# Windowed attention and a squared-ReLU product on one core: 192-token units up to token 3072, the rows of x turned by 128-row matmuls over zeros, the second product 15 units behind

## The chip, the core and the metric

One core of a Trainium2 chip runs the whole program. The metric is the device time of one execution in microseconds (us); the published number of a kernel is the median over its runs. The kernel before took 290.09 us (three runs: 293.07, 290.09, 288.38).

## What is computed

For 8 batches of 8 heads, 576 positions and head width 64, attention is taken within a window of 32 positions to either side, and its output, laid out as 4608 tokens of 512 features, goes through two matrix products with a squared ReLU between:

```
mask = np.abs(pos[:, None] - pos[None, :]) <= 32
scores = np.where(mask, q @ k.T / np.sqrt(D), -1e9)
attn = softmax(scores);  x = attn @ v          # x: 4608 tokens x 512
h = x @ w_in                                   # w_in: 512 x 2048
out = np.maximum(h, 0.0) ** 2 @ w_out          # w_out: 2048 x 512
```

## The kernel before, in words

**Attention** goes by groups of 192 positions, three to a batch and 24 in all (G = 0 to 23). A group's q, k and v rows are loaded by POOL's DMA queue with a cast to bf16; q and k are turned so that features lie on the partitions, by matmuls against the identity for G below 6 (`turn_pe`, L578) and by transposing DMAs on SP's queue from G = 6 on (`turn_dma`, L618). Scores are 24 small matmuls on half of the array's rows (L707; L659 for the first groups). ACT takes their exponentials (L721, L724), DVE multiplies by the band mask (L729 for the outer two of the three steps, L735 twice for the middle one), and two groups of eight matmuls (`pv`, L763) multiply by v, the first and the second window of the group. DVE divides by the sums (reciprocal L782, product L785), which gives `xa` (64 token rows, on partitions 64 to 127) and `xb` (128 token rows). `xa` is written in its lower half only; the partitions 0 to 63 of its buffers are never written.

**Turning x** (`xturn`, from L799). For G below 5 the token rows are turned on TensorE, and ACT copies the result to `xt` (L860): L843 turns `xa`, four matmuls of 64 rows by 64 columns, and L848 turns `xb`, four of 128 by 128. G = 0 has a form of its own (L811 to L838). From G = 5 on both are transposing DMAs on SP's queue (L864, L867), so each `xt` row passes two queues before the first product can use it: SP's, where it stands behind the q and k turns that were put there earlier, and the DMA engines'.

**First product** (`mm1`, L889). It goes by tiles of 192 tokens below token 2304 and of 256 tokens from there to 4096 (`TILES`); each tile is 64 matmuls over 16 blocks of `w_in` columns, two blocks to a PSUM bank. ACT applies ReLU (L895), and ACT or DVE squares (L905, L903) into `gt`. The last 512 tokens use a seven-product scheme (`mm1_tile`, `mm1_pair`, L966), for which `setup_w1s` (L922) prepares eight sums of `w_in` halves on DVE and writes them into the buffers that held raw k and q; such a write waits until the last transposing DMA that reads its buffer is done.

**Second product** (`mm2`, L1023; `mm2_pair`, L1083, a seven-product scheme over two blocks of 128 tokens) follows `LAGP` units of 64 tokens behind the first, and its sums go out by DMAs.

**What sets the order.** Each operation is recorded once with a key (its due place, in units of 64 tokens), a duration and what it reads and writes. `Prog.schedule` (L175) then plays the five engines and three DMA queues through a table of costs, takes the ready operation with the lowest key, and so fixes one static order for each engine. ACT or DVE is chosen for operations that have both forms (`alt`, with the offsets of `FLEX`). The keys get small random shifts (`SEEDS`, `NOISE`). Attention of group G is due at `pos(G)` (L471), 3G - 8 less `LGS` for each group after the sixth; the first product of token t0 is due at t0/64 - 1. In the planned gaps of the opening the scheduler places matmuls over zeros that nothing reads (L412). On the chip each engine runs its list in order, so an instruction that waits holds up all that stand behind it.

Of the kernel before, what the change touches and what calls it, by code (L numbers as in the profile page):

```python
# [7 lines left out]
ACTF = mybir.ActivationFunctionType  # L8
# [8 lines left out]
NBLK = NTOK // 128  # L17
# [12 lines left out]
GK = 7.0  # L30
# [4 lines left out]
TBK = 0  # L35
GDL = 1
# [11 lines left out]
LSLACK = 1200  # L48
# [21 lines left out]
LGS = 0.2  # L70
WLEAD = 3
TILES = ((192, 2304), (256, 4608))
SEEDS = (43876, 83318, 97513, 36951, 80411, 85349, 77111, 51195, 76437, 71531, 64050, 49961, 54177, 91158, 55691, 27992, 55556, 58548, 7419, 10134)
NOISE = 0.1
NBIAS = 1
PKEY = 0.2
# [12 lines left out]
LAGP = 14.0  # L89
PSTEP = 0.35  # L90
SLEAD = 1.0
MOE = -1
SQBEG = 576
ULATE = 26
# [3 lines left out]
OFFS = {'S': 2.5, 'M': -2.5, 'g': 2.25, 'Z': 3.25, 'N': -1.75, 'cc.': -3.0, 'u': -2.0, 'X': -0.5, 'r': -2.25, 'c': -1.0}  # L98
DLEAD = 0.3
TWKEY = 7  # L100
# [3 lines left out]
FLEX = {'g': -1.75, 'Z': -2, 'ev': 0.25, 'o': 4.75, 'p': 3.25, 'm': -1.5}  # L104
# [9 lines left out]
class Prog:  # L114
# [45 lines left out]
    def kind(self, op):  # L160
        n = op.name
        return "s" if n[0] == "S" or n[0] == "T" and n[-1] == "a" else "t" if n[0] == "t" else "v" if n[0] == "P" and "." not in n else ""
# [201 lines left out]
class Gen:  # L364
# [434 lines left out]
    def xturn(self, G):  # L799
        xa, xb = self.XA[G % 3], self.XB[G % 3]  # L800
        key = self.pos(G) + 0.5
        r = 192 * G % RING
        wr = [("xt", (3 * G + c) % (RING // 64)) for c in range(3)]
        if G < NXT:
# [35 lines left out]

            def f0(e):
                for j in range(4):
                    mm = e.transpose(ps[:, 192 * j:192 * j + 64], xa[64:128, 128 * j:128 * j + 128], self.ID[64:128, 64:128])  # L843
                return mm

            def f1(e):
                for j in range(4):
                    mm = e.transpose(pb[:, 192 * j + 64:192 * j + 192], xb[:, 128 * j:128 * j + 128], self.ID[:])  # L848
                return mm

            self.p.rec("PE", f0, reads=[("xa", G % 3), "id"], writes=bank, key=key, dur=110, name=f"T{G}a")
            self.p.rec("PE", f1, reads=[("xb", G % 3), "id"] + bank * (not two), writes=bank2, key=key, dur=230, name=f"T{G}b")
            if two:
                for x, (c0, c1) in enumerate(((0, 64), (64, 192))):
# [6 lines left out]
                                                     ps[:, 0:768].rearrange("p (j q) -> p j q", j=4), ACTF.Copy),  # L861
# [314 lines left out]
    def build(self):  # L1176
# [37 lines left out]
        def at(key, f, *a):  # L1214
            todo.append((key, len(todo), f, a))
# [22 lines left out]
        while t0 < NTOK:  # L1238
            if t0 in STR1:
                if t0 == STR1[0]:  # L1240
                    at(t0 / 64 - 2.5, self.setup_w1s, t0 / 64 - WLEAD)
                at(t0 / 64 - 2, self.mm1_tile, t0, t0 / 64 + MOE)
                for d in range(8):
                    at(t0 / 64 + d + MOE, self.mm1_pair, t0, d, t0 / 64 + d + MOE)
                t0 += 512
                continue
            n = next(n for n, end in TILES if t0 < end)
            m = min(512 // n, 4)
            for d in range(0, 16, m):
                key = t0 / 64 + d / 16 * n / 64 + MOE  # L1250
                at(key, self.mm1, t0, n, list(range(d, d + m)), key)
            t0 += n
        if NBLK - 2 not in PAIRS:
            at(500, self.mm2_last, NBLK - 1, 500)
        for u in PAIRS:
            key = 2 * u + LAGP - 4 * (u == NBLK - 2)
# [50 lines left out]
```

## Time and profile before

| | |
|---|---|
| published time | 290.09 us, median of 3 (288.38 to 293.07) |
| the profiled execution, its own time | 291.74 us |
| its span, first to last instruction | 289.9 us |
| granted TensorE clock | 1.00 |
| TensorE (PE) busy | 282.1 us, 97% |
| weight loads (PEld) busy | 245.2 us, 85% |
| VectorE (DVE) busy | 219.8 us, 76% |
| ScalarE (ACT) busy | 215.4 us, 74% |
| GpSimd (POOL) busy | 106.8 us, 37% |
| first matmul over zeros that nothing reads, their number | at 1.2 us, 32 |

A row of the timeline gives the start, the length, the engine, the line and the operation, `out<-in`, the tile shape, how many instructions were merged, and in square brackets how long the engine sat idle before and what it waited for. Matmuls overlap, so the length of a merged row contains the run-out of its last one; the distance from a row's start to the next row's start is what it took of PE. A row of the windows gives, for each engine, the busy time inside the stretch. "DVE L922" in a wait means that DVE's instruction at line 922 was what ended it; "issue" is a wait that the profile puts down to nothing it shows.

### The profile page before, as it was taken

To read this page: it belongs to the slowest core of one execution; us is meant where nothing else is said; L and a number is where in the kernel's file an instruction comes from. 1 tells how busy PE (TensorE), PEld (TensorE's weight loads), DVE (VectorE), ACT (ScalarE), POOL (GpSimd) and SP (SyncE) were. 2 spreads that over 40 slices of the span, in tenths; PEclk is the share of its full clock that TensorE was granted. 3 is DMA by queue.
4 is the path that set the end of the run, shared out by engine and by line. 5 is a ranking of instruction groups with operands and counts; after the bars stand their busy time and mean duration, and the time that the engine had idled before them with its cause. 6 is when DMAs were issued, how large, how long until landed. Compare 5 with 4: busy or idle time off the path is not lost.

```text
span 289.9 us, 8460 instructions
## 1 busy us (share of the span) xinstructions
PE 282.1 (97%) x3424; PEld 245.2 (85%) x3430; DVE 219.8 (76%) x472; ACT 215.4 (74%) x404; POOL 106.8 (37%) x143
## 2 busy tenths in 40 slices
PE   7998999999999999999999899999999999999996
PEld 2567988698899999999988788898889888888885
DVE  6668679969668978688866664987898857889863
ACT  3379999985489889688978898777887855788310
POOL 8985663260264664454665246425000000000000
PEclk9999999999999999999999999999999999999999
DMA  9999999999599999999999999999922030202124
GB/s 167 188 194 176 205 179 161 135 195 132 128 158 179 131 165 141 210 150 134 179 145 188 150 122 186 169 152 187 170 41 84 20 102 0 76 0 76 72 75 145
DMA packets 158983, 39.59 MB, mean 137 GB/s; under 512 B 148320, under 2 KB 154592, under 8 KB 158944
## 3 DMA queue, kind: packets, MB, share of 16 engines
q0 software_dynamic: 106016, 17.93, 89.8%
q1 hardware_dynamic: 47888, 12.07, 31.7%
q10 hardware_dynamic: 5040, 9.05, 10.0%
q8 instruction: 27, 0.44, 0.7%
q14 instruction: 12, 0.10, 0.1%
HBM read 36.70 MB, written 9.44 MB: 159 GB/s over the span
## 4 chain that ended last, share of the span: by engine, by line
PE 87%; DMA 5%; DVE 5%; ACT 2%; issue 1%; DVEq 0%
PE ht L889 32%; PE outp L1083 29%; PE at L1083 6%; PE at L763 4%; DMA xt<-xb 3%; PE at L707 3%; PE outp L1023 2%; PE at L966 2%; PE ht L966 2%; DMA oe<-in_q_dram 1%; PE outp L412 1%; PE outp L889 1%; PE at L889 1%; DVE kt L609 1%; PE at L578 1%
## 5 line engine op out<-in xcount | busy, mean ns | idle before, releaser
L889 PE MATMUL ht<-xt,w 128*128 128x192 bf16 (+1 forms) x1120 | 119.5, 256 | 0.7 <-DMA xt<-xb 0.7
L889 PEld LDWEIGHTS ht<-xt,w 128*128 128x128 bf16 x1120 | 96.6, 98 | 8.0 <-DMA xt<-xb 1.0
L895 ACT ACTIVATE rt<-ht 128x384 bf16<-128x384 f32 (+1 forms) x140 | 72.2, 529 | 21.7 <-PE ht L889 20.6
L905 ACT ACTIVATE gt<-rt 128x384 bf16<-128x384 bf16 (+1 forms) x122 | 67.1, 566 | 2.4
L536 POOL DMA_DIRECT2D v<-in_v_dram x48 | 38.3, 805 | 43.8 <-PE at L763 19.4
L487 POOL DMA_DIRECT2D kraw<-in_k_dram x36 | 28.1, 783 | 36.5 <-issue 14.6
L487 POOL DMA_DIRECT2D qraw<-in_q_dram x36 | 28.1, 782 | 10.3 <-PE ht L889 5.2
L1083 PE MATMUL outp<-w,gt 128*128 128x256 bf16 x224 | 29.0, 273 | 0.0
L1083 PE MATMUL outp<-tw,gt 128*128 128x256 bf16 x224 | 29.0, 273 | 0.0
L1083 PE MATMUL outp<-tw,ss 128*128 128x256 bf16 x224 | 28.9, 273 | 0.1
L1083 PEld LDWEIGHTS outp<-w,gt 128*128 128x128 bf16 x224 | 21.5, 98 | 2.6
L1083 PEld LDWEIGHTS outp<-tw,gt 128*128 128x128 bf16 x224 | 21.7, 98 | 2.3
L1083 PEld LDWEIGHTS outp<-tw,ss 128*128 128x128 bf16 x224 | 21.2, 98 | 2.7 <-DVE ss L1069 0.3
L721 ACT ACTIVATE e<-at 128x1024 bf16<-128x1024 f32 x21 | 21.4, 1021 | 2.1 <-PE at L707 1.9
L763 PE MATMUL at<-v,pt 128*128 128x66 bf16 x384 | 20.1, 194 | 0.5 <-DVE pt L735 0.5
L735 DVE TENSOR_TENSOR pt<-em,mask 64x512 bf16<-64x512 bf16 x42 | 17.6, 420 | 3.8 <-ACT em L724 2.4
L763 PEld LDWEIGHTS at<-v,pt 128*128 128x128 bf16 x384 | 17.9, 98 | 1.7 <-DVE pt L735 0.8
L903 DVE TENSOR_TENSOR gt<-rt 128x384 bf16<-128x384 bf16 (+1 forms) x30 | 11.4, 382 | 10.2 <-ACT rt L895 10.0
L729 DVE TENSOR_TENSOR pt<-e,mask 128x1024 bf16<-128x1024 bf16 x21 | 14.5, 691 | 5.4 <-ACT e L721 5.0
L1103 DVE TENSOR_TENSOR oe<-outp,uu 128x256 f32<-128x256 f32 (+1 forms) x28 | 15.4, 551 | 3.4 <-PE outp L1083 2.8
L785 DVE TENSOR_TENSOR xa<-at,rs 64x512 bf16<-64x512 f32 x24 | 16.7, 695 | 1.1
L785 DVE TENSOR_TENSOR xb<-at,rs 128x512 bf16<-128x512 f32 x24 | 16.5, 686 | 0.7
(151 smaller groups left out, 412.0 us busy)
## 6 DMA issues: line engine op xcount, KB each, us to landing
out_dram<-oe ACTq DMA_DIRECT2D x34, 256.0 KB, 4.6
qraw<-in_q_dram POOLq DMA_DIRECT2D x36, 96.0 KB, 7.3
w<-in_moe_w_in_dram POOLq DMA_DIRECT2D x4, 512.0 KB, 11.0
v<-in_v_dram POOLq DMA_DIRECT2D x16, 128.0 KB, 8.1
w<-in_moe_w_out_dram POOLq DMA_DIRECT2D x4, 512.0 KB, 17.6
v<-in_v_dram POOLq DMA_DIRECT2D x16, 96.0 KB, 7.3
kraw<-in_k_dram POOLq DMA_DIRECT2D x12, 112.0 KB, 7.2
kraw<-in_k_dram POOLq DMA_DIRECT2D x12, 96.0 KB, 7.4
```

Of the source, the lines that this page charges most:

```text
L487: self.p.rec("POOL", lambda e, j=j: e.dma_start(raw[0:h, j, :].rearrange("p (h d) -> p h d", h=8), s[:, j]), writes=[("raw", t, G % NRAW, ...
L536: self.p.rec("POOL", lambda e, j=j, lo=lo, hi=hi, k0=k0: e.dma_start(vt[lo - k0:hi - k0, j, :, 0:64], self.v[b, :, lo:hi, :].rearrange("h ...
L721: self.p.rec("ACT", lambda e: e.activation(e2[:], self.AT[:, 0:1024], ACTF.Exp, scale=0.125), reads=lo, writes=[("e", n)], key=key, dur=ac ...
L729: self.p.rec("DVE", lambda e: e.tensor_tensor(out, e2[:].rearrange("p (h s q) -> p h s q", h=8, s=2), mb, ALU.mult), reads=[("e", n), ("ma ...
L735: self.p.rec("DVE", lambda e, w=w, r=r, x=x, mm=mm: e.tensor_tensor(pt[x:x + 64, w, :, 0:64], e1[r:r + 64, :].rearrange("p (h q) -> p h q" ...
L763: mm = e.matmul(avp[:, c:c + VS], pt[:, 4 * (h % 2) + h // 2, :], vt[:, w, h, :], start=(w == 0 and y == 0), stop=True, skip_group_check=True)
L785: self.p.rec("DVE", lambda e: e.tensor_tensor(x[r0:128, :].rearrange("p (x y c) -> p x y c", x=2, y=4), av[:, :, :, 0:64], rb, ALU.mult), ...
L889: mm = e.matmul(ht[:, n * x:n * x + n], self.W1[:, ft, 128 * d:128 * d + 128], self.XT[:, ft, r:r + n], start=(ft == 0), stop=(ft == 3))
L895: self.p.rec("ACT", lambda e: e.activation(rt[:, 0:c], ht[:, 0:c], ACTF.Relu), reads=htag, writes=[("rt", k % 4)], key=key, dur=act(c), na ...
L905: alt=("ACT", lambda e: e.activation(gt[:, d0:d0 + len(ds), r:r + n], rr, ACTF.Square), act(c), "g")
L1083: mm = e.matmul(op[:, 256 * half:256 * half + 256], a[:, d, :], w[:, d, :], start=first and d == 0, stop=d == 7, skip_group_check=True)
L1103: self.p.rec("DVE", lambda e: e.tensor_tensor(out, src, other, ALU.add), reads=btags[bank] + rd, writes=wr, key=key + k * PSTEP - DLEAD, d ...
```

## The change

- `TILES` gives 192-token tiles up to token 3072, 256-token tiles from there to 4096. The 768 tokens from 2304 on are four tiles of 64 matmuls with 192 columns, where they were three tiles of 64 with 256 columns. A 192-token tile reads the rows of one group; a 256-token tile reads those of two.
- `TFULL`: for groups 1 to 4 `xa` is turned by four full matmuls of 128 rows by 128 columns, over all partitions, whose first 64 output columns are dropped. So that partitions 0 to 63 hold zeros, three operations (`xz0` to `xz2`) clear them once in the opening; in the order they stand on ACT, ahead of what was its first activation before.
- `LAGP` 15 for 14: the second product is due one unit later. `LGS` 0.15 for 0.2: attention is due a little later for late groups. `GK` 6.5 for 7: loads of groups from 12 on are due half a unit later. `WLEAD` 6.5 for 3: the sums of `w_in` halves are due earlier.
- New random shifts, offsets and choices between ACT and DVE. `SQBEG`, `ULATE`, `LAGS` and `KPL` come with values that choose nothing else than before.

```
-GK = 7.0
+GK = 6.5
+TFULL = True
+XZKEY = -5
-LGS = 0.2
-WLEAD = 3
-TILES = ((192, 2304), (256, 4608))
+LGS = 0.15
+WLEAD = 6.5
+TILES = ((192, 3072), (256, 4608))
-LAGP = 14.0
-PSTEP = 0.35
+LAGP = 15
+PSTEP = 0.45
...
+            c = 64 * TFULL
+
             def f0(e):
                 for j in range(4):
-                    mm = e.transpose(ps[:, 192 * j:192 * j + 64], xa[64:128, 128 * j:128 * j + 128], self.ID[64:128, 64:128])
+                    if TFULL:
+                        mm = e.transpose(ps[:, 192 * j:192 * j + 128], xa[:, 128 * j:128 * j + 128], self.ID[:])
...
-                    mm = e.transpose(pb[:, 192 * j + 64:192 * j + 192], xb[:, 128 * j:128 * j + 128], self.ID[:])
+                    mm = e.transpose(pb[:, 192 * j + 64 + c:192 * j + 192 + c], xb[:, 128 * j:128 * j + 128], self.ID[:])
...
-                                                     ps[:, 0:768].rearrange("p (j q) -> p j q", j=4), ACTF.Copy),
+                                                     ps[:, c:768 + c].rearrange("p (j q) -> p j q", j=4), ACTF.Copy),
...
+        for i in range(3 * TFULL):
+            x = self.XA[i][0:64, :]
+            at(-20, lambda i, x: self.p.rec("DVE", lambda e: e.memset(x, 0.0), reads=["zz"], writes=[("xz", i)], key=XZKEY + i, dur=200, name=f"xz{i}",
+                                            alt=("ACT", lambda e: e.activation(x, self.ZZ[0:64, :], ACTF.Copy), 490, "Z")), i, x)
```

Lines after 842 move by up to 14 (L889 becomes L898, L1083 becomes L1092, L922 becomes L931), those before it by 4 (L763 becomes L767).

The change moves instructions on all engines. Three places matter below. The first is PE behind the second `pv` group of G = 14. Before, the last rows ahead of the tile that starts at token 2560 (the last row here), which reads rows that this `pv` leads to:

```order
L889 MATMUL ht<-xt,w 128x256 x16
L1083 MATMUL outp<-tw,ss 128x256 x8
L763 MATMUL at<-v,pt 128x66 x8
L889 MATMUL ht<-xt,w 128x256 x16
L1083 MATMUL outp<-tw,ss 128x256 x8
L707 MATMUL at<-qt,kt 128x64 x24
L889 MATMUL ht<-xt,w 128x256 x8
L1083 MATMUL outp<-tw,gt 128x256 x8
L889 MATMUL ht<-xt,w 128x256 x16
```

and in the change, the rows that start with the second `pv` of G = 15 and end with the row whose last eight matmuls are the first of the tile at token 2688, the first there to read rows of G = 14:

```order
L767 MATMUL at<-v,pt 128x66 x8
L898 MATMUL ht<-xt,w 128x192 x8
L1092 MATMUL outp<-tw,ss 128x256 x8
L711 MATMUL at<-qt,kt 128x64 x24
L898 MATMUL ht<-xt,w 128x192 x16
L1092 MATMUL outp<-tw,ss 128x256 x8
L898 MATMUL ht<-xt,w 128x192 x8
L767 MATMUL at<-v,pt 128x66 x8
L898 MATMUL ht<-xt,w 128x192 x16
```

Between the second `pv` of G = 14 and the first matmul that needs its rows there stood 64 matmuls of 256 columns, 40 of the second product, two groups of scores and two of `pv`; now there stand 104 of 192 columns, 40 of the second product, two of scores and three of `pv`.

The second place is DVE at the second sum of `setup_w1s`, which writes the buffer that held raw k of G = 19. Before, it stood ahead of the masks of G = 18 (L729, L735):

```order
L903 TENSOR_TENSOR gt<-rt 128x2x256
L922 TENSOR_TENSOR kraw<-w 128x1024
L729 TENSOR_TENSOR pt<-e,mask 128x8x2x64
L735 TENSOR_TENSOR pt<-em,mask 64x8x64 x2
L543 COPY v<-v 64x8x64
L1103 TENSOR_TENSOR uu<-outp,uu 128x256
L782 RECIPROCAL rs<-at 64x8
```

and in the change:

```order
L912 TENSOR_TENSOR gt<-rt 128x2x192
L739 TENSOR_TENSOR pt<-em,mask 64x8x64 x2
L733 TENSOR_TENSOR pt<-e,mask 128x8x2x64
L1105 COPY uu<-outp 128x256
L931 TENSOR_TENSOR kraw<-w 128x1024
L786 RECIPROCAL rs<-at 64x8
L1112 TENSOR_TENSOR uu<-outp,uu 128x256
```

The sum now stands behind the masks and ahead of the reciprocal of the same group.

The third place is SP's queue between the turn of `xb` of G = 16 and the turn of `xa` of G = 17. Before:

```order
L867 DMA_TRANSPOSE xt<-xb1 128x4x128
L618 DMA_TRANSPOSE kt0<-kraw1 128x4x96 x2
L618 DMA_TRANSPOSE qt0<-qraw1 128x4x96
L618 DMA_TRANSPOSE qt0<-qraw2 128x4x96
L864 DMA_TRANSPOSE xt<-xa2 128x4x64
```

and in the change:

```order
L876 DMA_TRANSPOSE xt<-xb1 128x4x128
L622 DMA_TRANSPOSE kt0<-kraw1 128x4x96
L622 DMA_TRANSPOSE qt0<-qraw1 128x4x96
L873 DMA_TRANSPOSE xt<-xa2 128x4x64
L622 DMA_TRANSPOSE qt0<-qraw2 128x4x96 x2
L876 DMA_TRANSPOSE xt<-xb2 128x4x128
```

Two turns stand between them where there were four.

More of the change, by code (lines that the diff above doesn't have):

```diff
@@ L35 @@
 TBK = 0
+TFULL = True
+XZKEY = -5
+LAGS = 0.0
+KPL = 0
 GDL = 1
@@ L161, in kind @@
         n = op.name
-        return "s" if n[0] == "S" or n[0] == "T" and n[-1] == "a" else "t" if n[0] == "t" else "v" if n[0] == "P" and "." not in n else ""
+        return "s" if n[0] == "S" or n[0] == "T" and n[-1] == "a" and (not TFULL or n == "T0a") else "t" if n[0] == "t" else "v" if n[0] == "P" and "." not in n else ""
     def change(self, a, b):
@@ L1242, in build @@
                 at(t0 / 64 - 2, self.mm1_tile, t0, t0 / 64 + MOE)
-                for d in range(8):
-                    at(t0 / 64 + d + MOE, self.mm1_pair, t0, d, t0 / 64 + d + MOE)
+                for y in range(2):
+                    for d in range(0, KPL, 2):
+                        for d0 in (d, 8 + d):
+                            key = t0 / 64 + d / 2 - 2 + 0.2 * (d0 > 7) + MOE if y == 0 else t0 / 64 + 8 - KPL / 2 + d / 2 + 0.2 * (d0 > 7) + MOE
+                            at(key, self.mm1, t0 + 256 * y, 256, [d0, d0 + 1], key)
+                for d in range(KPL, 8):
+                    key = t0 / 64 + d - KPL / 2 + MOE
+                    at(key, self.mm1_pair, t0, d, key)
                 t0 += 512
```

24 lines of the change are left out of this document (13 added, 11 removed), and 2 rows, old and new, of the table OPENING.

## Prediction

> **What bounds the kernel now.** I read the page's busy line first, then the stretches, then PE's own waits.
>
> ```profile
> span 289.9 us, 8460 instructions
> PE 282.1 (97%) x3424; PEld 245.2 (85%) x3430; DVE 219.8 (76%) x472; ACT 215.4 (74%) x404; POOL 106.8 (37%) x143
> ```
>
> PE is busy in 97% of the span, and no other engine comes near. A busy PE is not yet an efficient one, so the next views ask where it is not busy, and why.
>
> ```profile
> 0.00:10.00 10.00, 8.20 (x31) 3.39 (x32) 5.83 (x32) 3.41 (x4) 9.03 (x16) 1.00 1.09 173
> 10.00:20.00 10.00, 9.19 (x120) 5.62 (x120) 7.08 (x15) 5.43 (x8) 8.61 (x12) 1.00 1.64 189
> 20.00:30.00 10.00, 9.19 (x139) 8.08 (x137) 8.42 (x19) 9.72 (x19) 6.08 (x9) 1.00 1.77 183
> ...
> 150.00:160.00 10.00, 9.66 (x119) 8.28 (x117) 7.66 (x17) 8.31 (x16) 6.78 (x9) 1.00 1.75 186
> 160.00:170.00 10.00, 9.60 (x119) 8.47 (x120) 6.01 (x14) 8.99 (x17) 4.25 (x7) 1.00 1.87 147
> ...
> 180.00:190.00 10.00, 9.52 (x118) 8.15 (x117) 9.35 (x21) 7.55 (x14) 5.09 (x7) 1.00 2.29 166
> ...
> 280.00:290.00 10.00, 7.14 (x66) 6.17 (x63) 3.32 (x7) 0.77 (x2) 0.00 (x0) 0.99 0.30 107
> ```
>
> After the start, the core and its columns are PE, PEld, DVE, ACT, POOL. Of 289.9 - 282.1 = 7.8 us without PE, the first 30 us hold 1.80 + 0.81 + 0.81 = 3.4, the end 2.8 (the last sums and their stores), the three stretches between 0.34 + 0.40 + 0.48 = 1.2; all others share 0.4. So behind the opening PE can gain little by better order: what it does, it does back to back. The waits name the places.
>
> ```profile
> PE at L843 <- DVE xb L785: 0.8, 1, 0.8
> PE ht L889 <- DMA xt<-xb: 0.7, 1, 0.7
> PE ht L578 <- DVE qraw L510: 0.6, 1, 0.6
> PE at L763 <- DVE pt L735: 0.5, 1, 0.5
> ```
>
> Each is a single wait: for q at the start, for the first turn of x at 26.9 us, and two in the middle, at 160.4 and 181.5. The change can take these and the price of PE's own work; nothing else is open.
>
> **The change part by part.** *192 for 256 columns.* What a matmul takes of PE, from rows of the chain:
>
> ```profile
> 29.55 1.32 PE ht L889 x16
> ...
> 171.50 1.75 PE ht L889 x16
> ```
>
> 1.32/16 = 82.5 ns for 192 columns, 1.75/16 = 109.4 ns for 256. The 768 tokens cost 256 x 82.5 = 21.1 us instead of 192 x 109.4 = 21.0: nothing to gain or lose (+0.1). All other first and second products keep number and shape, so PE's sum of work stands.
>
> *The wait for x at 160.4.*
>
> ```profile
> 146.26 0.42 PE L763 MATMUL at<-v,pt 128*128 128x66 bf16 x8
> ...
> 150.73 1.22 SPq L867 DMA_TRANSPOSE xt<-xb  x1
> ...
> 158.63 1.04 PE L1083 MATMUL outp<-tw,gt 128*128 128x256 bf16 x8
> ...
> 160.40 1.92 PE L889 MATMUL ht<-xt,w 128*128 128x256 bf16 x16 [0.74 <-DMA xt<-xb]
> ```
>
> The second `pv` of G = 14 (146.26) ends at 146.5. Its `xb` was issued at 150.73 and landed at 160.3, 13.8 us after. PE could have begun the tile of token 2560 at 158.63 + 8 x 0.109 = 159.50, 13.0 us after: 0.90 us lost. In the change the first tile that reads rows of G = 14 is that of token 2688. Ahead of it PE has, by the counts shown with the change, 104 x 0.0825 + 40 x 0.109 + 2 x 0.45 + 3 x 0.25 = 14.6 us of work behind that `pv` (a group of scores is 148.36 to 148.81, one of `pv` 146.26 to 146.52 in the timeline). If x takes the same 13.8 us, 0.8 us are to spare and the wait is gone: -0.9 (bounds -0.9 and 0).
>
> *The block on DVE at 180.*
>
> ```profile
> 179.74 0.69 DVE L922 TENSOR_TENSOR kraw<-w 128x1024 bf16<-128x1024 bf16 x1 [3.18 <-issue]
> ...
> 181.06 0.87 DVE L735 TENSOR_TENSOR pt<-em,mask 64x512 bf16<-64x512 bf16 x2
> ...
> 180.02 1.04 PE L889 MATMUL ht<-xt,w 128*128 128x256 bf16 x8
> 181.54 0.43 PE L763 MATMUL at<-v,pt 128*128 128x66 bf16 x8 [0.48 <-DVE pt L735]
> ```
>
> DVE stands 3.18 us at a sum whose buffer SP's turns of k still read, with the masks of G = 18 behind it; PE's `pv` comes 1.52 - 8 x 0.109 = 0.65 us late. In the change the masks stand ahead of that sum: -0.65 (bounds -0.65 and 0). Behind it now waits the reciprocal of the same group, so what is late next is `xa` of G = 18. The tile of token 3456's rows is far off, and I count nothing for it.
>
> *Next to be late.* The first 256-token tile is now that of token 3072, which reads `xa` of G = 17.
>
> ```profile
> 172.90 2.56 SPq L618 DMA_TRANSPOSE qt<-qraw  x2
> 175.56 1.31 SPq L864 DMA_TRANSPOSE xt<-xa  x1
> ...
> 183.55 1.04 PE L889 MATMUL ht<-xt,w 128*128 128x256 bf16 x8
> ...
> DMA to landing us min/median/max: 7.3/7.3/7.3
> ```
>
> It landed at 175.56 + 7.3 = 182.9, and the tile began at 183.55: 0.7 us to spare, 0.65 of it from the wait just removed. By the same count of PE's work the change leaves 10.3 us between the first `pv` of G = 17 and this tile, where there were 11.4. But two turns of SP's queue ahead of it are gone, 2.56 us for two in the row above. Between +1.1 (queue saves nothing) and 0 I take +0.3.
>
> *The turns of x for G = 1 to 4.*
>
> ```profile
> 32.02 1.49 PE L889 MATMUL ht<-xt,w 128*128 128x192 bf16 x16
> 33.44 0.29 PE L843 MATMUL at<-ident,xa 64*128 64x64 bf16 x4
> 33.65 0.40 PE L848 MATMUL at<-ident,xb 128*128 128x128 bf16 x4
> 33.89 0.82 PE L889 MATMUL outp<-xt,w 128*128 128x192 bf16 x8
> ```
>
> Sixteen matmuls take 1.32, here 1.42: going to 64 rows costs 0.10. The four of 64 rows take 0.21, the four full ones 0.24. Two full sets would take 0.48 where 0.10 + 0.21 + 0.24 = 0.55 stand: -0.07 a group, -0.3 in all. The bounds are -0.07 and, if the full set kept the 0.10, +0.03 a group: -0.3 to +0.1. The Trainium skill, page "TensorE: Matmul & The Clock Gate", section "Wait — 56ns, not 53.3ns?", has warm matmuls start N/2.4 GHz + 2.5 ns apart, which the 82.5 ns above meets. By that alone the wider turn costs 4 x (55.8 - 29.2) = 0.11 us a group, +0.4 in all, and the sum below would be 289.2 us for 288.5. That hangs on half-row turns starting 29 ns apart, and the row above shows 0.21/4 = 53 ns.
>
> *The three fills of zeros on ACT.*
>
> ```profile
> 4.95 0.63 ACT L507 ACTIVATE qraw<-oe 96x512 bf16<-96x512 f32 x1 [2.92 <-DMA oe<-in_q_dram]
> ```
>
> ACT idles from 4.95 - 2.92 = 2.03 on for the first load of q. Three fills of 512 columns, at the 0.63 us of the row beside them, take 1.9 and end at 3.9. The cover is this load; without it they would cost 1.9 on the first chain.
>
> *The opening otherwise.*
>
> ```profile
> 10.27 1.16 DVE L609 COPY kt<-outp 128x896 bf16<-128x896 bf16 x1 [1.88 <-PE outp L578]
> 11.41 0.50 DVE L522 COPY kraw<-tw 96x1024 bf16<-96x1024 bf16 x1
> ...
> 12.26 0.51 PE L578 MATMUL outp<-ident,kraw 96*128 96x96 bf16 x8 [0.16 <-DVE mask L445]
> ```
>
> DVE's order now copies this k (L522) in the idle 1.88 us ahead of the first `kt` copy, and the mask's last step is due earlier too, so PE's turn of k need not wait: -0.16 (bounds -0.16 and 0). The order has 31 matmuls over zeros for 32, so the scheduler plans the same holes.
>
> *ACT and DVE.*
>
> ```profile
> L895 ACT ACTIVATE rt<-ht 128x384 bf16<-128x384 f32 x88 | 41.6, 490 | 6.6 <-PE ht L889 6.3
> L905 ACT ACTIVATE gt<-rt 128x384 bf16<-128x384 bf16 x78 | 39.5, 530 | 1.4
> L895 ACT ACTIVATE rt<-ht 128x512 bf16<-128x512 f32 x52 | 30.6, 596 | 15.1 <-PE ht L889 14.3 <-PE at L763 0.5
> L905 ACT ACTIVATE gt<-rt 128x512 bf16<-128x512 bf16 x44 | 27.6, 631 | 1.1
> ```
>
> Thirty-two ReLUs of 0.490 replace 24 of 0.596: +1.4 us; squares alike, 32 x 0.530 - 24 x 0.631 = +1.8, spread over ACT and DVE. That is 3.2 us in about 45, where ACT is busy 8.3 to 9.0 of 10; it fits. Where ACT was busy 9.72 of 10 (20 to 30) PE lost 0.8 to `xb`; if ACT filled up, a like loss per 10 us, up to 3 us, would follow. I take 0. One unit more of lag and later attention move PE's work, not its amount: 0.
>
> The sum: +0.1 - 0.9 - 0.65 + 0.3 - 0.3 - 0.16 = -1.6, so a span of 289.9 - 1.6 = 288.3. This execution took 291.74 us in all, 1.65 above the median of the runs, so the median lies 0.2 above its span: I forecast 288.5 us.
>
> **The rivals.** *The waits only move: 290.1 us.* PE's work is the same, and a new static order with new random shifts has its own late places. For it: the margin at token 3072 is as thin as the two waits that go, and the new sum behind the masks of G = 18 still blocks DVE for as long as SP's turns take. Against: both removed waits have a plain cause that the new order lacks.
>
> *Slower: x lands late in the stage of 192-token tiles, 292.5 us.* Turned x spreads widely:
>
> ```profile
> DMA to landing us min/median/max: 2.5/7.0/9.6
> ```
>
> This is L867 over its 19 turns. Counting PE's work as above, from second `pv` to tile, the tiles of tokens 1152 to 1728 have 9.3 to 13.0 us in the change, 0.8 to 1.6 less than before. From `pv` to issue `xb` of G = 14 took 4.2, so x needs 4.2 + 9.6 = 13.8 at worst. Were all four to meet the worst they would lose 4.5 + 2.3 + 2.1 + 0.8 = 9.7 us; it decides from a landing of about 5 us on at the first and 9 at the last. With under half of that, 4 us, the sum is 288.5 + 4 = 292.5. For it: the slack shrinks there and turns run longer with more in flight. Against: no tile of that stage waited before.
>
> *Much faster: 285.1 us.* If PE's 3.4 us of idle time in the first 30 us went as well, 288.5 - 3.4 = 285.1. The order of the opening, with its 31 matmuls over zeros, says nothing of the kind.
>
> **How the numbers follow.** The forecast gets 0.48, the moved waits 0.28, late x 0.20, much faster 0.04. The unknown terms reach from -2.1 to about +3 round the span; single runs of the kernel before lie 1.7 below and 3.0 above their median. The range 286.2 to 292.6 takes in forecast, moved waits and most of late x. Two per cent, about what a measurement of this kernel can tell from no change, is 5.8 us: below 284.3 or above 295.9. Faster than that 0.03, most of the last case; slower 0.07, the worst third of late x; within 0.90.
>
> **What would show it.** Right: no PE wait on `xt` between 150 and 170 us and none on `pt` near 180, PE busy near 282 us less the fewer fillers, 82.5 ns a matmul up to token 3072, four-matmul turns at 0.24 us. A wait on `xt` at token 3072 above 1 us would break my +0.3. Waits of L898 on DMA `xt` between 75 and 125 us would make the slower rival; ACT above 9.7 of 10 with PE waiting for PSUM would show that the smaller units cost more than their columns.

## The result, and the profile after

| | before | after |
|---|---|---|
| median of the ten runs | 289.69 us (288.38 to 293.07) | 295.79 us (291.26 to 299.44) |
| the profiled execution, its span | 291.74, 289.9 us | 291.61, 289.7 us |
| PE busy | 282.1 us | 282.4 us |

The ratio after to before is 1.010 (95% interval 1.006 to 1.015). A second series of twelve gave a median of 294.76 (288.56 to 300.26) and a ratio of 1.000 (0.9965 to 1.0035). The ratios are formed from the executions near each kernel's fastest only, while every median here is over all of them; so the medians and the shares over 293 us, 16 of 24 executions of the changed kernel against 10 of 125 of the one before, carry what follows. The forecast was 288.5, at most 292.6: wrong.

The profiled execution of the changed kernel is one of the short ones, and in it the forecast's picture holds. Its busy line, the stretches and PE's waits:

```profile
span 289.7 us, 8623 instructions
PE 282.4 (97%) x3487; PEld 247.4 (85%) x3493; DVE 219.6 (76%) x475; ACT 218.3 (75%) x420; POOL 106.9 (37%) x143
...
150.00:160.00 10.00, 10.00 (x143) 9.48 (x141) 6.79 (x16) 8.67 (x18) 5.84 (x9) 1.00 1.80 176
160.00:170.00 10.00, 10.00 (x141) 9.43 (x139) 8.11 (x18) 9.58 (x22) 5.35 (x8) 1.00 1.82 131
...
180.00:190.00 10.00, 10.00 (x126) 8.85 (x124) 8.02 (x17) 9.25 (x18) 4.63 (x6) 1.00 1.91 153
190.00:200.00 10.00, 9.37 (x117) 7.95 (x115) 6.40 (x13) 6.95 (x13) 4.42 (x6) 1.00 1.80 180
```

```profile
PE outp L416 <- DVE zz L410: 1.2, 1, 1.2
PE at L850 <- DVE xb L789: 0.8, 1, 0.8
PE ht L898 <- ACT rt L904: 0.6, 1, 0.6
PE ht L582 <- DVE qraw L514: 0.6, 1, 0.6
```

The three stretches that had 9.66, 9.60 and 9.52 are full; the waits on `xt` and `pt` are gone. One new wait stands at 197 us, for a ReLU on ACT. The time is not in this execution. It shows in a long one: look2, a single execution of the same kernel, 298.23 us. Here are its busy line, the stretches from 140 to 200 us (the last three columns are the granted clock, the DMA share and GB/s) and the longest waits of PE behind the opening:

```profile
span 296.4 us, 8623 instructions
PE 282.2 (95%) x3487; PEld 247.0 (83%) x3493; DVE 219.8 (74%) x475; ACT 219.2 (74%) x420; POOL 106.8 (36%) x143
...
140.00:150.00 10.00, 8.98 (x129) 8.27 (x127) 5.83 (x12) 8.65 (x19) 4.15 (x7) 1.00 2.21 135
150.00:160.00 10.00, 9.54 (x135) 8.82 (x134) 6.73 (x16) 8.14 (x18) 5.21 (x7) 1.00 1.60 165
160.00:170.00 10.00, 9.63 (x136) 8.87 (x134) 7.71 (x17) 9.25 (x21) 4.79 (x8) 1.00 2.29 120
170.00:180.00 10.00, 9.03 (x125) 7.93 (x122) 6.01 (x13) 7.38 (x17) 6.08 (x8) 1.00 1.94 140
180.00:190.00 10.00, 6.05 (x64) 5.12 (x65) 5.61 (x13) 5.18 (x12) 0.71 (x1) 0.92 1.68 167
190.00:200.00 10.00, 10.00 (x116) 8.45 (x115) 6.57 (x13) 7.79 (x14) 3.92 (x6) 0.91 2.50 158
```

```profile
PE ht L898 <- issue: 4.3, 2, 3.8
PE ht L898 <- DMA xt<-xb: 1.4, 2, 1.0
...
PE at L711 <- DVE xb L789: 0.9, 1, 0.9
```

PE is busy as long as in the short execution (282.2 for 282.4) and idle 14.2 us for 7.3. The added idle time, 6.8 us, lies between 140 and 190 us: 5.7 of it are four waits at L898, the first product, and 0.9 is one at the scores (L711). The longest is put down to "issue", that is, to nothing the profile names; the landing of the turned rows names it. PE's rows around it, SP's turn of `xa` of G = 17, and that turn's landing, in the long execution:

```profile
182.35 1.04 PE L1092 MATMUL outp<-tw,ss 128*128 128x256 bf16 x8
187.24 1.03 PE L898 MATMUL ht<-xt,w 128*128 128x256 bf16 x8 [3.85 <-issue]
188.11 0.47 PE L767 MATMUL at<-v,pt 128*128 128x66 bf16 x8
188.39 3.54 PE L898 MATMUL ht<-xt,w 128*128 128x256 bf16 x16
191.77 1.04 PE L1092 MATMUL outp<-tw,gt 128*128 128x256 bf16 x8
...
176.31 1.79 SPq L873 DMA_TRANSPOSE xt<-xa  x1
...
DMA to landing us min/median/max: 10.8/10.8/10.8
```

and in the short one:

```profile
181.12 1.04 PE L898 MATMUL ht<-xt,w 128*128 128x256 bf16 x8
...
172.66 1.19 SPq L873 DMA_TRANSPOSE xt<-xa  x1
...
DMA to landing us min/median/max: 5.3/5.3/5.3
```

The turn is issued 3.7 us later and takes 5.5 us longer: it lands at 187.1, and PE starts the unit of token 3072 at 187.24. In the short execution it lands at 178.0, 3.2 us ahead of need. From the same rows for every unit, the time between the last landing of x and the first matmul that reads it, in us:

| unit of token | 1536 | 1920 | 2304 | 2496 | 2688 | 2880 | 3072 | 3328 |
|---|---|---|---|---|---|---|---|---|
| after, short (289.7) | 4.2 | 3.8 | 5.5 | 5.8 | 6.8 | 4.7 | 3.2 | 3.7 |
| after, long (296.4) | 2.3 | 1.8 | 0.1 | 0.1 | 0.1 | 0.1 | 0.1 | 4.1 |

At 0.1 the unit starts when its rows land.

That the two spans differ by nearly the same 6.7 us is partly chance, since two other differences almost cancel. Behind the long wait sixteen matmuls that else take 1.75 us took 3.38 (188.39 to 191.77), 1.6 us more, at a granted clock near one half. And the short execution lost 1.8 us in the opening, where its matmuls of 512 columns ran at a slower pace, 2.98 us for seven against 1.76. First the short execution, then the long one:

```profile
6.43 3.19 PE L416 MATMUL outp<-zz 128*128 128x512 bf16 x7
9.41 0.95 PE L582 MATMUL outp<-ident,kraw 112*128 112x112 bf16 x8
```

```profile
6.16 1.68 PE L416 MATMUL outp<-zz 128*128 128x512 bf16 x7
7.92 0.57 PE L582 MATMUL outp<-ident,kraw 112*128 112x112 bf16 x8
```

The granted clock reads 1.00 there in both, so the traces do not say why. PE starts the unit of token 0 at 19.4 us in the short execution and at 17.6 in the long one, which up to token 1920 asks for its rows 1.8 us sooner.

SP's queue shows how a late load becomes a late x. SP issues one turn after another: the 60 turns that it starts between 85 and 175 us take it 83 of these 90 us in the short execution. So a turn of k whose rows have not landed holds back all turns behind it, those of x too, and SP has little idle time to catch up. In the long execution:

```profile
SPq L622 <- DMA kraw<-in_k_dram: 4.6, 2, 3.4
```

With 1.6 us booked under another line, SP waits 6.2 us there for loads of k between 60 and 200 us; in the short execution it waits for none. Two of the 6.2 us fall between 115 and 119 us, 3.4 only at 187. At 65 us SP was 1.8 us ahead of the short execution, at 121 us it is 2.7 behind; the other half of that loss is issues that took longer. In the nine profiles below and above that are over 293 us, SP waits for loads of q or k for 2.2 (b_gate) to 9.5 us (again), in the others for 0 to 1.4, but for 4.5 in late. So the question is why loads and turns are late, and what in the change did it.

### The profile page after: what moved, and what is told of

Read it like the earlier page. It is cut to its first block, busy times and chain, and to the rows that moved or that the text cites. A ratio compares the mean times of both kernels' runs of the same rounds, so it can differ in the third digit from the quotient of the medians.

```text
span 289.7 us, 8623 instructions
## 1 busy us (share of the span) xinstructions
PE 282.4 (97%) x3487; PEld 247.4 (85%) x3493; DVE 219.6 (76%) x475; ACT 218.3 (75%) x420; POOL 106.9 (37%) x143
## 4 chain that ended last, share of the span: by engine, by line
PE 90%; DVE 3%; ACT 3%; DMA 1%; ACTq 1%; issue 1%
PE ht L898 34%; PE outp L1092 29%; PE at L1092 6%; PE at L767 4%; PE at L711 3%; PE outp L1032 2%; PE ht L975 2%; PE at L975 2%; PE outp L416 2%; DMA oe<-in_q_dram 1%; PE outp L898 1%; PE at L898 1%; ACTq L1140 1%; PE at L582 1%; ACT qt L610 1%
## 5 line engine op out<-in xcount | busy, mean ns | idle before, releaser
L898 PE MATMUL ht<-xt,w 128*128 128x192 bf16 (+1 forms) x1184 | 119.4, 251 | 0.7 <-ACT rt L904 0.6
L898 PEld LDWEIGHTS ht<-xt,w 128*128 128x128 bf16 x1184 | 99.1, 98 | 6.0 <-ACT rt L904 0.9
L914 ACT ACTIVATE gt<-rt 128x384 bf16<-128x384 bf16 (+1 forms) x120 | 63.9, 551 | 2.6 <-ACT rt L904 0.3
L1092 PE MATMUL outp<-tw,gt 128*128 128x256 bf16 x224 | 29.0, 273 | 0.0
L1092 PE MATMUL outp<-w,gt 128*128 128x256 bf16 x224 | 29.0, 273 | 0.0
L1092 PE MATMUL outp<-tw,ss 128*128 128x256 bf16 x224 | 28.2, 273 | 0.0
L1092 PEld LDWEIGHTS outp<-w,gt 128*128 128x128 bf16 x224 | 21.6, 98 | 2.5
L1092 PEld LDWEIGHTS outp<-tw,gt 128*128 128x128 bf16 x224 | 21.5, 98 | 2.4
L1092 PEld LDWEIGHTS outp<-tw,ss 128*128 128x128 bf16 x224 | 21.2, 98 | 2.4
L739 DVE TENSOR_TENSOR pt<-em,mask 64x512 bf16<-64x512 bf16 x42 | 17.6, 420 | 5.5 <-ACT em L728 4.4
L912 DVE TENSOR_TENSOR gt<-rt 128x384 bf16<-128x384 bf16 (+1 forms) x40 | 14.5, 366 | 8.6 <-ACT rt L904 7.9
L767 PE MATMUL at<-v,pt 128*128 128x66 bf16 x384 | 20.1, 194 | 0.0
L767 PEld LDWEIGHTS at<-v,pt 128*128 128x128 bf16 x384 | 17.7, 98 | 1.8 <-issue 0.5
## 6 DMA issues: line engine op xcount, KB each, us to landing
w<-in_moe_w_out_dram POOLq DMA_DIRECT2D x4, 512.0 KB, 17.6
```

Of the source, the lines that this page charges most:

```text
L739: self.p.rec("DVE", lambda e, w=w, r=r, x=x, mm=mm: e.tensor_tensor(pt[x:x + 64, w, :, 0:64], e1[r:r + 64, :].rearrange("p (h q) -> p h q" ...
L767: mm = e.matmul(avp[:, c:c + VS], pt[:, 4 * (h % 2) + h // 2, :], vt[:, w, h, :], start=(w == 0 and y == 0), stop=True, skip_group_check=True)
L898: mm = e.matmul(ht[:, n * x:n * x + n], self.W1[:, ft, 128 * d:128 * d + 128], self.XT[:, ft, r:r + n], start=(ft == 0), stop=(ft == 3))
L914: alt=("ACT", lambda e: e.activation(gt[:, d0:d0 + len(ds), r:r + n], rr, ACTF.Square), act(c), "g")
L1092: mm = e.matmul(op[:, 256 * half:256 * half + 256], a[:, d, :], w[:, d, :], start=first and d == 0, stop=d == 7, skip_group_check=True)
```

## The experiments

**Is it the kernel, and is it the full-row turns?** Nothing altered, and the turns alone undone in an otherwise identical order on every engine:

```
-  mm = e.transpose(ps[:, 192 * j:192 * j + 128], xa[:, 128 * j:128 * j + 128], self.ID[:])
+  mm = e.transpose(ps[:, 192 * j + 64:192 * j + 128], xa[64:128, 128 * j:128 * j + 128], self.ID[64:128, 64:128])
```

> The changed kernel once more, nothing altered. The profile shown for it has TensorE without the two waits and a span of 289.7 us, yet the median of its runs was 295.8. Theory A (late transfers): most executions have some stages in which rows of x, turned rows of k and q or blocks of v land later than in the profile shown, and TensorE waits 1 to 5 us at a few places; then the median is again 294 to 297 and the profile of a long execution shows waits of TensorE for a DMA that the profile shown does not have. Theory B (granted clock): the same executions show no more waits, but a granted clock under 1.00 for some stretch, and matmuls of 82.5 ns at 192 columns longer there. Theory C: the long executions were of that one chip; then the median here is 290 to 292.

> The changed kernel in its very same order on every engine, with one thing undone: the rows of x of groups 1 to 4 are turned as before by 64-row matmuls of 64 columns instead of 128-row matmuls over zeros (the zero fills stay). If the full-row turns cost what makes the change long (theory D), this one is shorter than the changed kernel by 3 us or more. If late transfers or the order do it (theory A), it is within 1 us of the changed kernel and has the same spread between executions; the forecast's price of the full-row turns (-0.3 us) makes it 0.3 us longer.

> The changed kernel again, one execution and its profile, so that an execution of 294 us or more can be seen beside one of 291. Theory A: waits of TensorE for DMAs (rows of x at the first expert product of 192-token units, turned q or k at the scores) add up to what it is over 291. Theory B: no added waits, a granted clock under 1.00 instead.

> As the look before: one more execution of the changed kernel. If both executions are over 293 us, theory A expects their added waits at the same places in the order (the same groups of rows); theory B expects the granted clock to be low in the same stretch.

Measured: 294.76 us, 7 of 12 over 293; without the full-row turns 294.60, 8 of 12 (before beside them: 289.46, 1 of 23). look1 took 293.75, with one wait of 2.2 us at the unit of token 3072 and the clock at 1.00; look2 is the long execution above. Late transfers (A) hold, the lower clock (B) comes behind them, C and D fall: the turns cost nothing that shows.

**Is it the lag, or the 192-token units?** The order is planned anew in these three:

```
lag14      -LAGP = 15                               +LAGP = 14.0
units2304  -TILES = ((192, 3072), (256, 4608))      +TILES = ((192, 2304), (256, 4608))
b_lag15    -LAGP = 14.0                             +LAGP = 15        (in the kernel before)
```

> The changed kernel with one number back: the second product 14 instead of 15 units behind, all else (192-token units to 3072, full-row turns, weights of the order) as changed. The DMA engines are shown 9 tenths busy or more from the start to 190 us in every profile, and in the changed kernel TensorE starts the units of tokens 1536 to 3584 2 to 4 us earlier than before (103.9 for 105.8, 181.1 for 183.6), so x is needed sooner while the transfers go at the same pace. Theory L (the lag pulls transfer-fed work forward): here the units start 1 to 2 us later than in the changed kernel, the waits for turned x shrink, and the median falls from 295 to 289 to 292 with few executions over 293. Theory S (the 192-token units up to 3072 do it): no change, median 294 to 296.

> The changed kernel with the 192-token units only up to token 2304, as before; the lag of 15 and the rest stay. Theory L: still long, median 293 to 297, with waits for x of 1 us and more at the 256-token units from 2304 on (a 256-token unit needs its last rows of x sooner than a 192-token one). Theory S: the median falls to 289 to 291.

> The kernel before with the lag alone set to 15. Theory L: longer than before, median 291 to 296, with TensorE waiting for turned x between 140 and 190 us in the profile. Theory S, or a third one (the weights and seeds of the order as a whole): within 1 us of before, 288.5 to 290.5.

Measured (before beside them 289.76, 4 of 35 over 293): lag14 293.84, 7 of 12; units2304 291.09, 3 of 12, with five executions from 288.16 to 288.53 and six from 292.50 up; b_lag15 291.20, 1 of 12, without a wait for x. Theory L fell twice: the lag set back does not mend the changed kernel, set forward it does not bring the waits. The median of b_lag15 lies in theory L's range, but not for L's reason: its profile has one added wait, of 1.7 us, at 275 us and for DVE. The units matter, some 4 us in the median, but they are not all of it, since half of the executions of units2304 stay long. What these orders differ in can be counted: second-product matmuls (L1083, L1092) done ahead of the first matmul of the unit at token 1728. In the profiles of before and after:

```profile
0.00:117.60 117.60, 29.76 (x240) 22.76 (x240) 1.00 1.68 164
```

```profile
0.00:113.70 113.70, 26.02 (x208) 19.59 (x208) 1.00 1.70 165
```

240 of them in 117.6 us against 208 in 113.7: all else that PE did up to there is the same to nine matmuls (1472 against 1431 in all). lag14 has 184 (110.5 us), units2304 208, b_lag15 240. The planner, whose keys were all shifted, fills PE differently; the lag's number is only one of its inputs. The count goes with the time only loosely: units2304 has the 208 of the changed kernel and is 4 us shorter, and lag14 with the fewest is not the longest. The next runs intervene.

**Do transfers bind at all?** The order kept, a part of the loads of v left out:

```
-  vt[lo - k0:hi - k0, j, :, 0:64], self.v[b, :, lo:hi, :] ...
+  vt[lo - k0:hi - k0, j, 0:8 if G < 9 else 4, 0:64], self.v[b, 0:8 if G < 9 else 4, lo:hi, :] ...
```

> The changed kernel in its very same order, but from the tenth group of 192 rows on the loads of v bring 4 of 8 heads (the other heads keep older rows, so this leaves out part of the attention's data): about a sixth of the packets on the loads' queue from 79 us on is gone. Theory A (the transfers are at their limit, and whatever is slow in them makes TensorE wait): loads of q and k land 6 to 7 us after issue instead of 9 to 10, no wait of TensorE for x at all, median 287.5 to 289.5 and a spread under 2 us. If the waits come from SP's order rather than from the DMA engines' pace: still 294 to 296.

Measured: 289.16 (288.57 to 290.19), 0 of 12 over 293, ratio 0.9996 (0.9972 to 1.0019); loads of q land 5.1 us after issue, SP waits for none, and PE has no wait on `xt`. That settles the kind of cause: with lighter loads the whole excess goes.

**Does PE come too early for them?** Useless work for PE ahead of the stretch, in the same order:

```
-  for x, d in enumerate(ds):
+  for x, d in list(enumerate(ds)) * (1 + (t0 == 1152 and d0 < 10)):
```

> The changed kernel in its very same order, with 40 first-product matmuls of the unit at token 1152 done twice (their first results are overwritten by the same values): 40 times 82.5 ns, 3.3 us of useless TensorE work at 83 us, ahead of the stretch in which the transfers fall behind. Theory P (in the changed order TensorE reaches the unit of token 1728 at 113.7 us for 117.6 before, with 32 second-product matmuls fewer behind it, 208 for 240, so rows of q, k, v and x are wanted 3 to 4 us sooner than the DMA engines bring them): the added work gives the transfers that time back, the waits for turned x shrink, and the median is 291 to 294, below the changed kernel's 294.8, with the low end at 288.6 + 3.3 = 291.9. If the waits have nothing to do with how far TensorE is ahead of the transfers, 3.3 us come on top: median 298.

Measured: 292.28, five of six between 291.88 and 293.31, one at 297.57 (before 289.05). Adding 3.3 us to the busiest engine shortened the median by 2.5, from 294.76 in an earlier set of runs; before moved by 0.4 between the two sets. The profile is of the one long execution. Its largest wait is not for x, but 2.3 us at the scores, for DVE:

```profile
PE at L711 <- DVE xb L789: 2.3, 1, 2.3
```

```profile
177.48 0.69 DVE L931 TENSOR_TENSOR kraw<-w 128x1024 bf16<-128x1024 bf16 x1 [3.51 <-DMA kt<-kraw]
```

DVE stands 3.5 us at the first sum of `setup_w1s`, whose buffer a late turn of k still reads, with `xb` of G = 17 and the scores behind it. In the short execution this sum does not wait. The 0.9 us at L711 in the long execution above, 1.3 us in gate, the one long wait of late's profile (2.0 us) and that of lag14's (2.6 us, at a later sum) are of the same kind.

**Earlier or later loads.** Each load of q, k and v has, besides its buffer's own hazards, a throttle: it waits for an attention product of an earlier group. The order is kept, and only that wait is moved. `gate` and `b_gate`:

```
+  if op.eng == "POOL" and op.dma is not None and op.dma[0][0] in "qkv" and op.dma[1] > 9:
+      g = self.named[GATE.format(op.dma[1] - GD - GDL)]
+      if g in op.deps:
+          op.deps.discard(g)
+          op.deps.add(self.named[GATE.format(op.dma[1] - GD - GDL - 1)])
```

> The changed kernel in its very same order on every engine; only the throttle of the loads of q, k and v from the tenth group on is one group earlier (a load waits for the second attention product of the group five before it instead of four; the waits for its own buffer stay). Before the stretch in question GpSimd issues no load from 67 to 79 us, and the DMA engines' share falls to 0.8 of 10 there. Theory P: with loads issued in that gap the transfers gain up to 10 us of lead, the waits for turned x go, median 287.5 to 290 and a spread under 3 us. If the DMA engines' pace is not what is short there, or if earlier loads only stand in the way of the turns: 294 or more, the turns landing 9 us and more after issue.

> The kernel before with the same one edit on the throttle of the loads. Its profile shows two waits on that side (0.9 us for turned x at 160 us, 0.65 at 181). Theory P: these go, median 1 to 1.6 us below before, 287.5 to 289. If earlier loads stand in the way of the turns: 290 or more.

> The kernel before, nothing altered, one execution and its profile, to see how the same transfers run there. Theory P: loads of q and k land 6 to 8 us after issue, TensorE reaches the unit of token 1728 at 116 to 118 us, and no wait for x over 1.5 us. If an execution of this kernel has loads at 10 us and waits like those of the changed kernel, the difference between the kernels is one of how often this happens, not of whether.

Two things in these expectations were wrong. The column they read as a share of 10 is the packets' time summed over the queues, in units of the 16 engines' time: 1.6 to 2.3 in the tight stretch, 0.8 in the gap. And groups 10 and 11, whose loads follow that gap, wait for first products and not for the gate's attention products, so the edit left the gap as it was and moved only the loads from group 12 on.

Measured: gate 294.66 (294.39 to 294.98, 6 of 6 over 293), b_gate 294.25 (5 of 6), before 289.05 (0 of 11); b_look 290.56, its unit of token 1728 at 116.1 us, with one wait of 1.7 us for x where none over 1.5 was expected. Loads issued earlier into queues that were already full made gate long in all of its six executions and b_gate in five. In the lists of DMAs (KB, then the median from issue to landing), the changed kernel's short and long executions:

```profile
qraw<-in_q_dram POOLq DMA_DIRECT2D x36, 96.0 KB, 6.7
...
xt<-xb SPq DMA_TRANSPOSE x19, 6.5
```

```profile
qraw<-in_q_dram POOLq DMA_DIRECT2D x36, 96.0 KB, 9.8
...
xt<-xb SPq DMA_TRANSPOSE x19, 8.1
```

and gate:

```profile
qraw<-in_q_dram POOLq DMA_DIRECT2D x36, 96.0 KB, 15.3
...
xt<-xb SPq DMA_TRANSPOSE x19, 7.7
```

Loads that stand longer in their queue go with turns that take longer in theirs, though not evenly (8.1 us at 9.8, 7.7 at 15.3) and not always: in again's profile, the longest of all with a span of 298.4 us, loads of q take 9.6 us and turns of `xb` 5.6, and x is late there because SP issues its turns late, some 6 us behind the short execution's from 147 us on. The loads were then issued earlier where the queues are empty (hole, b_hole), and, the other way, later from group 12 on (late):

```
hole, b_hole
+  if op.eng == "POOL" and op.dma is not None and op.dma[0][0] in "qkv" and op.dma[1] in (10, 11):
+      op.deps = (op.deps - op.raw) | {self.named[GATE.format(op.dma[1] - 5)]}
late
+  if op.eng == "POOL" and op.dma is not None and op.dma[0][0] in "qkv" and op.dma[1] >= GFAR:
+      op.deps = (op.deps - op.raw) | {self.named["P{}A".format(op.dma[1] - 3)]}
```

> The changed kernel in its very same order; only the loads of q, k and v of groups 10 and 11 are issued earlier (they wait for the second attention product of group 5 and 6, at 66 and 75 us, instead of first products at 79 and 86 us), which fills the gap in which the DMA engines idle (0.8 of 10 from 70 to 80 us). From group 12 on the throttle is as it was, so the loads' queue gets no deeper than in the changed kernel. Theory P (the transfers lack the 3 to 4 us by which TensorE runs ahead in the changed order): 12 loads done ahead of the tight stretch give them that back, the waits for turned x shrink to under 2 us, median 288.5 to 291. Theory Q (what slows the turns is how deep the loads are queued, whatever the lead): the queue is as deep as before from 92 us on, so the median stays at 293 to 296.

> The kernel before with the same edit on the loads of groups 10 and 11. Theory P: its two waits (0.9 us for x at 160 us, 0.65 at 181) shrink, median 0.5 to 1.5 us under before. Theory Q: 289 to 290, as before, or up to 293 where the earlier loads leave a deeper queue behind.

> The changed kernel in its very same order; the loads of q, k and v from group 12 on wait for the first attention product of the group three before, about 5 us later than now, so that fewer of them stand in the queue at a time. Theory Q: loads land 5 to 6 us after issue, turns of x 5 to 6 us after theirs, the waits for turned x at 145 to 190 us shrink, median 288.5 to 291 and few over 293. Theory P without Q: loads 5 us later take the last slack (turns of q and k start 0 to 6 us after their rows land), TensorE waits more, median 296 or more.

(late also numbers the semaphores ahead of the loop, since its loads wait for operations that are recorded behind them.) The stretch from 70 to 80 us, in the changed kernel and with the gap filled:

```profile
70.00:80.00 10.00, 10.00 (x127) 8.79 (x125) 7.19 (x15) 4.61 (x10) 0.61 (x1) 1.00 0.81 145
```

```profile
70.00:80.00 10.00, 10.00 (x137) 8.91 (x135) 6.95 (x15) 5.18 (x11) 4.41 (x7) 1.00 1.98 176
```

The DMA share goes from 0.81 to 1.98. Measured: hole 290.36 (289.02 to 293.29, 1 of 12 over 293), ratio 1.0033 (1.0004 to 1.0062); b_hole 289.08 (288.19 to 290.47, 0 of 12), ratio 0.9990 (0.9966 to 1.0014); late 292.71, 3 of 6; before 289.62, 3 of 23. Theory P has its number: twelve loads out of the way ahead of the tight stretch take 4.4 us off the median of the same order (294.76 in the earlier set; before moved by 0.2). In hole's profile SP waits for no load, and one wait for x is left:

```profile
PE ht L901 <- DMA xt<-xb: 0.5, 1, 0.5
```

For theory Q late has the sign, with a median between what the two theories gave. In its profile, the shortest of its six at 291.03, loads land sooner and turns run faster:

```profile
qraw<-in_q_dram POOLq DMA_DIRECT2D x36, 96.0 KB, 6.2
...
xt<-xb SPq DMA_TRANSPOSE x19, 5.2
```

but of the first 14 turns of q and k behind 84 us, eight start within 0.7 us of the landing of their rows (three in the changed kernel's short execution), and half of the executions stay over 293. For b_hole the medians differ by 0.5 us and the interval holds 1: no gain is shown.

**A version that beats both, and what the order is worth without transfers.** units2304 with hole's edit; and the kernel before with light_v's edit:

> The kernel with the 192-token units to 2304 and the rest as changed (median 291.1, its shortest executions 288.2, the longest 295.4), with the loads of groups 10 and 11 issued into the idle gap as in the run that brought the changed kernel from 295 to 290.4. Theory P: the executions of 292 to 295 us go, median 288.2 to 289.5, at or below both kernels. If not, 290 to 292.

> The kernel before with the loads of v cut as in the lighter changed kernel (4 of 8 heads from the tenth group on; it leaves out part of the attention's data). It shows what the change is worth where transfers do not bind: the lighter changed kernel was 289.2 with before at 289.8 beside it. If the forecast's terms on TensorE alone hold (256-column matmuls of 109.4 ns for 192-column ones of 82.5, the turns, the opening: -0.36 us in all, and two waits of 1.55 us that lighter loads take from this kernel too), this one is 288.2 to 289.5, within 0.7 us of the lighter changed kernel. If it is 287.5 or less, the changed order costs TensorE time of its own.

Measured beside before at 289.09 (1 of 23 over 293): hole_2304 289.58 (288.92 to 294.85, 1 of 12), ratio 1.0019 (0.9991 to 1.0046): the executions over 293 go but for one, and what is left is no shorter than before: I have no version that beats both. b_light_v 288.99 (288.31 to 290.77), ratio 0.9995 (0.9972 to 1.0018); light_v had 0.9996. Where transfers do not bind, the two orders take the same time.

## Why the prediction was wrong

**The columns: right.** PE is busy 282.4 us for 282.1, +0.1 forecast.

**The two waits: right as far as they went.** Both are gone from the short execution, and the order of DVE at 180 works as described there. In long executions the same kind of block comes back at the first of these sums (2.1 us of DVE in look2). And the two waits were worth nothing in the median: b_light_v loses its transfer waits too and stands at before's own median, so typical executions of before did not pay the 1.55 us of the one profiled. That one was 1.65 us above the median with a slow opening besides: its unit of token 0 starts at 19.4 us, that of b_look at 17.7. One execution was a poor base to subtract from.

**Turns and opening: too small to see.** The turns' -0.3 had bounds of -0.3 to +0.1; half_turns is 0.16 us off, inside the spread. In the trace the sixteen matmuls ahead of one group's turns take 1.32 us and the two sets 0.23 and 0.22, together 0.10 less than before, where -0.07 was forecast. The wait for the mask is gone, but one of 0.3 us for `qt` has come (L663), and the opening's three stretches keep 3.5 us of idle time for 3.4, so the -0.16 did not come through. The fills of zeros are hidden as said: they end at 3.7 us, ahead of the load.

**The bounds.** Those listed term by term add up to -1.9 and, with the 3 us for ACT, to +4.3, not to -2.1 and about +3; the range ended below its own worst case.

**The step that failed: "One unit more of lag and later attention move PE's work, not its amount: 0."** The amount is the same, and moving it is not free. It is the whole order that moved, not the lag's number, as lag14 shows. With 32 second-product matmuls (3.5 us at 0.109) less ahead of the unit of token 1728, PE asks for rows of q, k, v and x sooner between 95 and 185 us (units start 1.9 us earlier at token 1536, 3.9 at 1728, 0.2 at 1920, 3.0 at 2304, 2.4 at 3072, by the two profiles with the same slow opening), while loads and turns come at the pace they had: SP's turns fill 83 or 84 of the 90 us from 85 to 175 in both. In the median that costs 5 to 6 us, where 0 was put. delay gave that time back and hole brought transfers forward; both took most of the excess off. I had taken each landing as a given of its turn (7.3, 13.8 us), from one execution, and asked only whether PE's work behind it still covers it.

**The same error, at token 3072.** "Between +1.1 (queue saves nothing) and 0 I take +0.3" was bounded by the queue's length. It is the worst place of the long executions: 3.85 us in the one shown, 2.2 in look1, 5.6 in again. The queue was two turns shorter, but all of it came late. My mark for it, a wait above 1 us, was met.

**The slower rival had the mechanism and not the place or the size.** x lands late in the 192-token stage, but not at tokens 1152 to 1728, where 2 us and more were left in the long execution, but at 2304 to 3072. Its 292.5 was 4 us of waits; the medians say 5 to 6. It had 0.20, and the moved waits, which is what a new order does when transfers are taken as fixed, had 0.28.

**What stays open.** Why the same program runs the stretch easily in one execution and with full queues in the next was not settled: the long execution moves 152 GB/s from 85 to 190 us and the short one 164, but PE's waits hold loads back too, so cause and effect are not told apart. The opening's pace alone does not decide it: look1 and half_turns have the slow one and long waits, hole and light_v the fast one and no wait for x above 0.5 us. Whether the limit is SP's issuing or the DMA engines was not tried either: light_v leaves SP as full as it was (85 of the 90 us) and still has no wait. Nor was each number of the planner tried alone; that the moved balance of second products is what matters is argued from delay and hole, and the counts of five orders do not bear it out by themselves. delay and hole were also not run beside the changed kernel, only beside before.

## What to carry to other kernels

When an order is changed on an engine that is 97% busy, ask first how far it runs ahead of its transfers: work that is only postponed pulls fed work forward, and queues near their limit turned 2 to 4 us of lead into 5 to 6 us of the median here. Count the engine that issues transfers like any other: SP, busy 83 of 90 us, did not make up in the long execution what it had lost. Judge margins of landings by their spread over several executions, and look for a gap where the queues stand empty ahead of a full stretch: loads moved there helped, while loads added to full queues hurt. Where medians and profile disagree, profile again until a long execution is caught.

## What the runs showed of the hardware

Turns on SP's queue mostly take longer where loads on GpSimd's stand longer. Medians from issue to landing, loads of q and turns of `xb`: 5.1 and 5.2 us (light_v), 6.2 and 5.2 (late), 6.7 and 6.5 (after, short), 9.8 and 8.1 (after, long), 15.3 and 7.7 (gate), 17.1 and 8.1 (b_gate), but 9.6 and 5.6 in again. The Trainium skill, page "DMA: Bandwidth & Descriptors", section "Queues, rings and completion order", has each DMA engine go round the queues that have work, one packet at a time. Medians up to about 8 us fit a turn that pays for loads in the other queue, but again does not, and no run here shows the packets taking turns.

A wait of TensorE can cost twice. In the stretches of the long execution above the granted clock is 0.92 and 0.91 around and behind the 3.85 us wait, and sixteen matmuls take 3.38 us for 1.75; in again's profile, after a wait of 5.6 us, the clock (the third number from the right) is

```profile
188.00:190.00 2.00, 1.82 (x11) 1.33 (x12) 0.00 (x0) 0.00 (x0) 0.00 (x0) 0.50 0.88 162
190.00:192.00 2.00, 2.00 (x18) 1.47 (x16) 1.48 (x4) 1.23 (x2) 0.81 (x2) 0.50 0.28 57
192.00:194.00 2.00, 2.00 (x11) 1.40 (x10) 0.48 (x1) 1.30 (x3) 2.00 (x3) 0.52 0.98 89
194.00:196.00 2.00, 2.00 (x39) 1.61 (x38) 0.85 (x2) 1.81 (x3) 1.81 (x3) 1.00 1.70 135
```

half for about 6 us, though PE counts as busy there. A wait of 2.2 us left it at 1.00 in look1; one of 2.1 us was followed by 0.70 over 185 to 190 us in half_turns.
